# Moving the later gate columns behind the weight conversion in a fused mLSTM and bilinear kernel

## The chip, the cores and the metric

The kernel runs on one core of a Trainium2 chip. The number that counts is the device time of one execution in microseconds (us). The kernel before takes 566.85 us, the median of three runs (566.21 to 568.91).

The engines are named as in the profile: PE (matrix multiplications), DVE, ACT and POOL (elementwise work), and SP, whose queue issues the DMAs here. Each engine works through its own list of instructions in order; semaphores make one wait for another.

## The reference

Two steps are fused. The first is a recurrent attention with exponential gates over 4 batch rows, 8 heads, 768 time steps and a head size of 40. The second takes its output as 3072 tokens of 320 numbers through a bilinear layer with 1536 hidden columns.

```python
for t in range(S):
    m_new = np.maximum(f_gate[:, :, t] + m, i_gate[:, :, t])
    f_stab = np.exp(f_gate[:, :, t] + m - m_new)
    i_stab = np.exp(i_gate[:, :, t] - m_new)
    C = f_stab * C + i_stab * outer(v_t, k_t)
    n = f_stab * n + i_stab * k_t
    y_t = sigmoid(o_gate_t) * (C @ q_t) / max(|n . q_t|, 1)
x = y as (3072, 320)
out = (x @ w_a * (x @ w_b)) @ w_out
```

The three weight matrices arrive as 64-bit floats, everything else as 32-bit floats.

## The kernel before

**Chunks.** Time is cut into six pieces of 128 steps. A chunk is one piece of one batch row, so there are 24; chunk n is piece n // 4 of batch row n % 4. Within a chunk the recurrence is a masked matrix product: scores from q and k (`pS`), multiplied by a decay matrix E (tile `gbc`), times v (`pV`); from piece 1 on, the state that earlier pieces left (`cst`) is added (`pI`, `num`). The state is brought up to date by `weigh` (POOL: v times a column of weights w, tile `vw`) and `stage_u` (PE: `pU`). `stage_f` divides and applies the output gate (tile `osig`), and `stage_d` transposes the result (`pX`) into `xh` and `xl`, a high and a low part, which the bilinear layer reads.

**Gates.** `first_gates` works out the gate sums of the first 128 columns, at the kernel's start. `later_gates` does columns 128 to 767: a scan for the running maximum, three elementwise passes over 32 x 640 numbers, five scans for the running sums G, the tables beta and w, transposes on PE (`ptg`) into `gtab`, an Exp over part of it, and `dec`. G also goes to DRAM (`g_dram`), from which `load_g` spreads one chunk's rows over 128 partitions as the raw E of chunks 4 and later; POOL masks it (`affine_select`), and ACT takes eight Exps with a column of `gtab` as bias (`stage_e`). Chunks 0 to 3 build E on PE instead (`begin_e`, `pE`) and need no `gtab`, except for the column w in `weigh`.

**Weights.** The 64-bit weights come in 32 pieces ("stages" x = 0 to 31). For each one ACT makes a high part (`high`), DVE a low part (`low`) and their union (`join`), ACT rounds it (`lead_part`), and DVE subtracts (`low_part`): three DVE and two ACT instructions, or one more of each for the pieces 4, 12, 20 and 28. Hidden columns come in 12 groups ff; group ff needs eight stages for every three groups (`need`).

**Blocks.** The bilinear layer takes the chunks in nine blocks of two or three chunks. A block is twelve times `up(ff)` (16 matmuls into two `pu` accumulators) and `down(ff)` (three matmuls per chunk into `pd`), with g, gh and gl between them on DVE, ACT and POOL. `run_block(kb)` writes block kb's matmuls and in between, at a pace set by `units` over `total`, the attention of the chunks that block kb + 1 needs. During block 0 the conversion of the stages 5 to 31 is written too, one step for every four matmuls.

**What sets the order.** Chunks 0 and 1 and the stages 0 to 4 are written out by hand. Blocks 0 and 1 are ordered for all engines by the scheduler at build time; from block 2 on, PE and SP follow the written order. In `rest()` the written order is: two steps of `later_gates`, the transposes and E of chunk 2, the rest of `later_gates`, then `weigh` and `stage_u` of chunks 0 and 1, then the attention.

## Time and profile before

| | |
|---|---|
| runs | 568.91, 566.21, 566.85 us; median 566.85 |
| profiled execution | 564.22 us |
| its span, from the first to the last instruction | 562.4 us |
| mean granted PE clock | 0.969 of full speed |
| busy: PE, DVE, ACT, POOL | 534.6, 411.9, 221.3, 126.6 us |

The profile gives for each instruction its start, its length and, where the engine was idle before it, for how long and what released it. Matmul ends are modelled, so that a stretch can count as busy on PE though its clock was low; the granted clock stands beside it.

### The profile page before, as it was taken

The page shows a single profiled execution, that of the slowest core. Times are in us where ns is not written, and L with a number is a line of the kernel's source. Part 1 is how long each engine was busy: PE and PEld are TensorE (multiplying, and loading weights), DVE is VectorE, ACT ScalarE, POOL GpSimd, SP SyncE. Part 2 cuts the span into 40 slices and gives each one's busy share as a digit, 9 for nine tenths or more (in the row PEclk, how much of TensorE's full clock was granted, in tenths as well). Part 3 has the DMA queues.
Part 4 walks back from the last instruction along what each step waited for, and adds up shares of the span by engine and source line. Part 5 has one row for each costly group of instructions (what it writes and reads, how often), then busy time and mean ns, then how long its engine had stood idle before and what let it go on. Part 6 is the DMA issues. An engine that isn't in the chain of part 4 may idle for free.

```text
span 562.4 us, 12436 instructions
## 1 busy us (share of the span) xinstructions
PE 534.6 (95%) x4810; PEld 505.9 (90%) x4810; DVE 411.9 (73%) x967; ACT 221.3 (39%) x530; POOL 126.6 (23%) x185
## 2 busy tenths in 40 slices
PE   9678799997999999999999999999999999899997
PEld 6576699997999989999899999899999999799997
DVE  6899976468879965978859995978859577744342
ACT  5677854344422642332632441541432515111111
POOL 2012245253331230332132231233030202100000
PEclk9587789999999999999999999999999999999999
DMA  9999513567956955677855654967544834200001
GB/s 172 300 273 303 110 38 89 117 95 160 153 135 105 167 119 76 146 142 158 139 119 119 120 108 106 190 121 155 89 122 75 139 76 114 35 1 24 2 0 36
DMA packets 198679, 66.77 MB, mean 119 GB/s; under 512 B 184252, under 2 KB 191900, under 8 KB 198620
## 3 DMA queue, kind: packets, MB, share of 16 engines
q1 hardware_dynamic: 198620, 65.98, 57.8%
q8 instruction: 38, 0.62, 0.5%
q14 instruction: 21, 0.17, 0.1%
HBM read 41.11 MB, written 5.97 MB: 84 GB/s over the span
## 4 chain that ended last, share of the span: by engine, by line
PE 68%; DVE 5%; DMA 5%; issue 4%; ACT 3%; SPq 2%; POOL 1%; POOLq 0%; ACTq 0%; DVEq 0%
PE pu L744 39%; PE pd L716 18%; PE pV L520 3%; PE pS L468 2%; PE pU L544 2%; DMA osig<-in_o_gate_dram 1%; ACT gbc L413 1%; PE pX L630 1%; PE pS L818 1%; PE pI L494 1%; PE pV L870 1%; DMA T<-qks 1%; SPq L160 1%; DMA gbc<-g_dram 1%; DMA qk<-in_q_dram 1%
## 5 line engine op out<-in xcount | busy, mean ns | idle before, releaser
L744 PE MATMUL pu<-xh,w 128*128 128x384 f32 (+1 forms) x1080 | 282.5, 328 | 3.9 <-DVE w L373 2.2
L744 PE MATMUL pu<-xl,w 128*128 128x384 f32 (+1 forms) x648 | 210.7, 327 | 1.0 <-DVE xl L636 1.0
L744 PEld LDWEIGHTS pu<-xh,w 128*128 128x128 f32 x1080 | 194.1, 192 | 7.1 <-DVE w L373 3.4
L716 PE MATMUL pd<-w,gh 128*128 128x320 f32 x576 | 132.8, 315 | 1.0 <-ACT gh L754 1.0
L744 PEld LDWEIGHTS pu<-xl,w 128*128 128x128 f32 x648 | 124.7, 193 | 2.0 <-DVE xl L636 1.3
L716 PEld LDWEIGHTS pd<-w,gh 128*128 128x128 f32 x576 | 97.9, 190 | 1.6 <-ACT gh L754 1.2
L752 DVE TENSOR_TENSOR g<-pu,g 128x384 f32<-128x384 f32 (+1 forms) x108 | 54.6, 505 | 56.7 <-PE pu L744 53.7
L716 PE MATMUL pd<-w,gl 128*128 128x320 f32 x288 | 89.2, 315 | 0.0
L751 ACT COPY g<-pu 128x384 f32<-128x384 f32 (+1 forms) x92 | 40.5, 440 | 114.4 <-PE pu L744 114.1
L413 ACT ACTIVATE gbc<-gbc,gtab 128x128 f32<-128x128 f32 x160 | 49.4, 389 | 23.8 <-POOL gbc L406 23.8
L455 POOL TENSOR_TENSOR vr<-va 128x336 f32<-128x336 f32 x18 | 14.0, 775 | 187.1 <-PE pV L520 176.6
L716 PEld LDWEIGHTS pd<-w,gl 128*128 128x128 f32 x288 | 53.8, 189 | 0.0
L756 DVE TENSOR_TENSOR gl<-g,gh 128x384 fp32r<-128x384 f32 (+1 forms) x92 | 50.3, 546 | 1.6
L754 DVE CAST gh<-g 128x384 fp32r<-128x384 f32 (+1 forms) x96 | 32.7, 341 | 1.6
L475 ACT CAST pb<-gbc 128x512 bf16<-128x512 f32 x36 | 22.2, 616 | 26.7 <-DVE gbc L473 26.6
L527 DVE TENSOR_TENSOR num<-pV,num 128x336 f32<-128x336 f32 x18 | 9.1, 504 | 29.9 <-PE pV L520 29.9
L406 POOL TENSOR_SCALAR_AFFINE_SELECT gbc<-gbc 128x1024 f32<-128x1024 f32 x20 | 23.7, 1185 | 18.9 <-DMA gbc<-g_dram 17.1
L562 ACT CAST cb<-cst 128x168 bf16<-128x168 f32 x18 | 6.0, 331 | 54.6 <-DMA gbc<-g_dram 26.7
L473 DVE TENSOR_TENSOR gbc<-pS,gbc 128x512 f32<-128x512 f32 x36 | 24.5, 680 | 3.6 <-PE pS L468 3.6
L520 PEld LDWEIGHTS <-pb 128*128 128x128 bf16 x576 | 23.1, 96 | 4.2 <-DVE pb L479 1.8
L607 POOL TENSOR_TENSOR osig<-osig,den 128x320 f32<-128x320 f32 x22 | 17.0, 771 | 43.8 <-DVE den L602 25.4
L431 ACT CAST qks<-qk 128x320 bf16<-128x320 f32 x36 | 16.1, 452 | 27.3 <-DMA T<-qks 12.4
(130 smaller groups left out, 814.1 us busy)
## 6 DMA issues: line engine op xcount, KB each, us to landing
gbc<-g_dram SPq DMA_DIRECT2D x20, 512.0 KB
qk<-in_q_dram SPq DMA_DIRECT2D x24, 160.0 KB
qk<-in_k_dram SPq DMA_DIRECT2D x24, 160.0 KB
va<-in_v_dram SPq DMA_DIRECT2D x24, 160.0 KB
osig<-in_o_gate_dram SPq DMA_DIRECT2D x24, 160.0 KB
raw<-in_moe_w_out_dram SPq DMA_DIRECT2D x12, 320.0 KB
out_dram<-o SPq DMA_DIRECT2D x24, 160.0 KB
raw<-in_moe_w_a_dram SPq DMA_DIRECT2D x8, 384.0 KB
```

The costliest lines, as they stand in the source:

```text
L406: nc.gpsimd.affine_select(E, E, pattern=[[0, H], [1, P]], compare_op=ALU.is_ge, fill=-1e30, base=0, channel_multiplier=-1,)
L413: nc.scalar.activation(E[:, h], E[:, h], AF.Exp, bias=beta[:, h:h + 1])
L473: nc.vector.tensor_tensor(E, pS, E, op=ALU.mult)
L475: nc.scalar.copy(pb[:, 0], E)
L520: nc.tensor.matmul(pv[:, h], pb[i][:, h % HH, :], vb[j][:, h], start=(x == 0), stop=(x == len(terms) - 1),)
L607: (nc.vector if n < NS else nc.gpsimd).tensor_tensor(yv, yv, den.unsqueeze(2).broadcast_to([P, H, D]), op=ALU.mult)
L716: nc.tensor.matmul(pd[t][:, 0:DM], a[:, cols], w, start=(ff == 0 and first), stop=(ff == NF - 1 and last),)
L744: up_in = nc.tensor.matmul(acc[j], a, r, start=(x == 0), stop=(x == len(terms) - 1),).ins
L751: (nc.vector.tensor_copy if kb > 0 and ff in [1, 2] else nc.scalar.copy)(g, acc[0])
L752: nc.vector.tensor_tensor(g, acc[1], g, op=ALU.mult)
L754: (nc.vector.tensor_copy if kb > 0 else nc.scalar.copy)(gh, g)
L756: (nc.gpsimd if kb * 12 + ff < 16 else nc.vector).tensor_tensor(gl, g, gh.bitcast(F32), op=ALU.subtract)
```

## The change

The column w of chunks 0 to 3 gets a small table of its own, `w0tab` (128 x 32), worked out in the hand-written part by `first_weights`: one DVE add, one PE transpose, one Exp on ACT. With it `weigh` of chunks 0 and 1 is written before block 0, into two buffers of the tag `vr`, which is idle until chunk 6; `weigh` of the other early chunks uses the same two buffers instead of the single buffer `vw`. `later_gates` leaves `rest()` and is written at the head of chunk 3 in `early_chunk`, after stage 25 of the conversion (`need(26)`), with `load_g` of chunk 4 behind it. It no longer handles the first piece: no copies of its two rows on ACT, five pieces to DRAM instead of six, five transposes instead of six; the Exp over `gtab` is split in two, a small one for piece 1's decay column a and one for the rest. The Sigmoids of two output gates move into chunk 2. Block 0 writes a conversion step for every three matmuls, and starts its attention eight units later.

```diff
+    w0tab = wpool.tile([P, BH], F32, name="w0tab")
...
+    def first_weights():
+        w0 = gf[:, 0:P]
+        nc.vector.tensor_scalar(w0, gb3[0][:, 1], gb3[0][:, 0, P - 1:], None, op0=ALU.add)
+        pw = ps_dn.tile([P, 512], F32, tag="pd2", name="pw")[:, 0:BH]
+        nc.tensor.transpose(pw, w0, ident[0:BH, 0:BH])
+        nc.scalar.activation(w0tab, pw, AF.Exp)
...
-        with tc.issue_after(start["dve"]):
+        with tc.issue_after(after["dve"]):
             nc.vector.tensor_tensor_scan(m, f, i, gm[:, P - 1:P], op0=ALU.add, op1=ALU.max)
...
-        with tc.issue_after(start["act"]):
-            nc.scalar.copy(G[:, 0], gb3[0][:, 0])
-            nc.scalar.copy(tab[BH:2 * BH, 0], gb3[0][:, 1])
...
-            nc.sync.dma_start(g_dram.rearrange("c g t -> g c t"), G)
+            nc.sync.dma_start(g_dram[1:].rearrange("c g t -> g c t"), G[:, 1:])
...
-            for c in range(n3):
+            cs = range(max(half * n3, 1), (half + 1) * n3)
+            for x, c in enumerate(cs):
...
+        nc.scalar.activation(a_col(1, 0, B), a_col(1, 0, B), AF.Exp)
+        x = gtab[:, 4 * BH:].rearrange("p (c g) -> p c g", g=3 * BH)[:, :, 0:2 * BH]
         nc.scalar.activation(x, x, AF.Exp)
...
     def w_col(c, b):
-        return g_col(c, b, 1)
+        return g_col(c, b, 1) if c > 0 else w0tab[:, b * H:(b + 1) * H]
...
     def early_chunk(n):
+        if n == NS + 1:
+            need(26)
+            yield from later_gates()
+            load_g(NE)
         aside("L", n)
...
         yield from (begin_e if n + 1 < NE else stage_e)(n + 1)
+        if n == NS:
+            for b in range(NS, B):
+                squash(0, b, 1)
...
-        vw = apool.tile([P, H, DV], F32, tag="vw", name=f"vw{n}", bufs=1)
+        vw = apool.tile([P, H, DV], F32, tag="vr", name=f"vw{n}")
...
         run(E[1], 2)
+        first_weights()
...
+        for n in range(NS):
+            weigh(n)
...
     def rest():
-        gates = later_gates()
-        for _ in range(2):
-            next(gates)
-            yield
-        yield from begin_a(NS)
-        yield from begin_e(NS)
-        yield from gates
         for n in range(NS):
-            weigh(n)
             yield from stage_u(n)
             if n == 0:
                 with tc.issue_after(issued["w"]):
                     load(NS + 1)
-        for b in range(2, B):
-            squash(0, b, 1)
-        load_g(NE)
+        yield from begin_a(NS)
+        yield from begin_e(NS)
         yield from attention()
...
+        lead_in = 8 if kb == 0 else 0
+        acc = -lead_in
...
-            if x % (4 if kb == 0 else 6) == 0:
+            if x % (3 if kb == 0 else 6) == 0:
                 next(conv, None)
-            acc += units / (total * (0.93 if kb < 2 else 0.88))
+            acc += (units + lead_in) / (total * (0.93 if kb < 2 else 0.88))
```

Three places show what this does to the order on the engines. The line numbers of the changed kernel are higher by five to twelve; the operations are the same.

**DVE at the start of block 0**, while the stages 5 to 9 are converted (`cw` and `w`: conversion; `T_1`: the copy of chunk 2's transposed k; `qks_91`: the gate rows; `g_0`: block 0). Before:

```order
L220 TENSOR_TENSOR qks_91<-qks_91 32x640
L222 TENSOR_TENSOR qks_91<-qks_91 32x640
L354 SCALAR_TENSOR_TENSOR cw<-qks_89,cw 128x320
L354 SCALAR_TENSOR_TENSOR cw<-qks_90,cw 128x320
L354 SCALAR_TENSOR_TENSOR cw<-qks_89,cw 128x384
L373 TENSOR_TENSOR w_473<-cw,w_473 128x320
L808 COPY T_1_492<-pT_1_493 128x512
L221 TENSOR_TENSOR qks_91<-qks_91 32x640
L752 TENSOR_TENSOR g_0_470<-pu_0_1_449,g_0_470 128x256
```

Now:

```order
L359 SCALAR_TENSOR_TENSOR cw<-qks_90,cw 128x320
L359 SCALAR_TENSOR_TENSOR cw<-qks_89,cw 128x320
L359 SCALAR_TENSOR_TENSOR cw<-qks_90,cw 128x320
L359 SCALAR_TENSOR_TENSOR cw<-qks_89,cw 128x384
L378 TENSOR_TENSOR w_474<-cw,w_474 128x320
L820 COPY T_1_590<-pT_1_591 128x512
L764 TENSOR_TENSOR g_0_478<-pu_0_1_458,g_0_478 128x256
L378 TENSOR_TENSOR w_489<-cw,w_489 128x320
```

The elementwise passes over 32 x 640 gate numbers are gone from here. They now stand among the conversion of the last stages, and the five scans for G stand behind the subtraction of stage 29 (`w_983`), with two subtractions of the conversion still to come:

```order
L229 TENSOR_TENSOR qks_91<-qks_91 32x640
L359 SCALAR_TENSOR_TENSOR cw<-qks_89,cw 128x320
L378 TENSOR_TENSOR w_957<-cw,w_957 64x384 x2
L359 SCALAR_TENSOR_TENSOR cw<-qks_90,cw 128x320
L378 TENSOR_TENSOR w_983<-cw,w_983 128x320
L233 SCALAR_TENSOR_TENSOR qks_92<-one,qks_91 32x128 x5
L641 TENSOR_TENSOR xl_1041<-pX_1042,xh_1040 128x3x128
L820 COPY T_1_1117<-pT_1_1118 128x512
```

**POOL at the end of block 0** (`gl`: low part of g of one group; `osig`: output gate of chunk 2 or 3 times the reciprocal; `gbc`: the mask on a loaded E). Before, the mask there is that of chunk 5:

```order
L756 TENSOR_TENSOR gl_8_1194<-g_8_1159,gh_8_1192 128x256
L607 TENSOR_TENSOR osig_159<-osig_159,den_1122 128x320
L406 AFFINE_SELECT gbc_1022<-gbc_1022 128x1024
L756 TENSOR_TENSOR gl_9_1257<-g_9_1238,gh_9_1255 128x256
L455 TENSOR_TENSOR vr_1619<-va_86 128x336
```

Now it is that of chunk 4 (`gbc_1005`), and the output gate of chunk 3 and the last `gl` of block 0 stand behind it:

```order
L768 TENSOR_TENSOR gl_10_1299<-g_10_1286,gh_10_1297 128x256
L398 MEMSET qks_91 128x8x8 x2
L411 AFFINE_SELECT gbc_1005<-gbc_1005 128x1024
L612 TENSOR_TENSOR osig_160<-osig_160,den_1179 128x320
L768 TENSOR_TENSOR gl_11_1330<-g_11_1317,gh_11_1328 128x256
L411 AFFINE_SELECT gbc_1103<-gbc_1103 128x1024
```

The rows moved are the masks of chunks 4 and 5. In the kernel before, chunk 4's stands far earlier, between gl_3 and the weighted v of chunk 1.

**PE and ACT at the change from block 0 to block 1** (`pd`: block 0's `down`; `pu_0_0`: block 1's first accumulator; `pI`, `pX`, `pT`: attention). PE before:

```order
L716 MATMUL pd_0_446<-w_1243,gh_10_1294 128x320 x2
L716 MATMUL pd_0_446<-w_1243,gl_10_1296 128x320
L716 MATMUL pd_1_447<-w_1243,gh_10_1294 128x320 x2
L716 MATMUL pd_1_447<-w_1243,gl_10_1296 128x320
L805 MATMUL pT_0_1395<-ident,qk_82 128x128 x3
L744 MATMUL pu_0_0_1355<-xh_933,w_302 128x256
L805 MATMUL pT_0_1395<-ident,qk_82 128x128
L744 MATMUL pu_0_1_1356<-xh_933,w_435 128x256
```

PE now:

```order
L728 MATMUL pd_1_456<-w_1031,gh_11_1328 128x320 x2
L830 MATMUL pS_1_1199<-T_0_1105,T_1_1117 128x128 x4
L728 MATMUL pd_0_455<-w_1031,gl_11_1330 128x320
L728 MATMUL pd_1_456<-w_1031,gl_11_1330 128x320
L260 MATMUL ptg<-ident,qks_92 128x96 x3
L270 MATMUL pdec<-ends,sides 128x64
L851 MATMUL pI_0_1222<-cst_93,T_0_1105 128x42 x4
L851 MATMUL pI_1_1223<-cst_93,T_0_1105 128x42 x4
L635 MATMUL pX_1243<-ident,osig_160 128x128 x3
L549 MATMUL pU_1152<-vw_1127,qk_80 64x42 x8
L817 MATMUL pT_0_1398<-ident,qk_82 128x128 x4
L756 MATMUL pu_0_0_1358<-xh_1040,w_303 128x256
```

Before, block 1's first `up` matmuls stand ahead of the last `pd` rows, and `pI` of chunk 4 and `pX` of chunk 3 further ahead still. Now `pu_0_0` stands behind the whole of block 0, the transposes of the gate table, `pI` and `pX`. ACT before, around chunk 5's Exps (`gbc_1022`) and the cast of chunk 3's `xh`, which block 1 reads:

```order
L413 ACTIVATE gbc_1022<-gbc_1022,gtab 128x128 x8
L751 COPY g_10_1283<-pu_10_0_1273 128x256
L431 CAST qks_91<-qk_81 128x8x40
L754 CAST gh_10_1294<-g_10_1283 128x256
L634 CAST xh_933<-pX_1206 128x3x128
L751 COPY g_11_1314<-pu_11_0_1304 128x256
L754 CAST gh_11_1325<-g_11_1314 128x256
```

ACT now:

```order
L266 ACTIVATE gtab<-gtab 128x32
L418 ACTIVATE gbc_1005<-gbc_1005,gtab 128x128 x8
L436 CAST qks_91<-qk_81 128x8x40
L418 ACTIVATE gbc_1103<-gbc_1103,gtab 128x128 x2
L738 COPY o_0_1350<-pd_0_455 128x320
L418 ACTIVATE gbc_1103<-gbc_1103,gtab 128x128
L738 COPY o_1_1353<-pd_1_456 128x320
L418 ACTIVATE gbc_1103<-gbc_1103,gtab 128x128 x4
L268 ACTIVATE gtab<-gtab 128x4x64
L418 ACTIVATE gbc_1103<-gbc_1103,gtab 128x128
L274 ACTIVATE dec<-pdec 128x64
L639 CAST xh_1040<-pX_1243 128x3x128
```

The cast of chunk 3's `xh` now stands behind the eight Exps of chunk 4 (`gbc_1005`), the eight of chunk 5 (`gbc_1103`), block 0's output copies and the Exps of the gate tables.

More of the change, by code (lines that the diff above doesn't have):

```diff
@@ L245, in later_gates @@
         nc.vector.tensor_tensor(
-            tab[2 * BH:], tab[BH:2 * BH], G[:, :, P - 1:P].broadcast_to([BH, NC, P]), op=ALU.add
+            tab[2 * BH:, 1:], tab[BH:2 * BH, 1:], G[:, 1:, P - 1:P].broadcast_to([BH, NC - 1, P]),
+            op=ALU.add,
         )
@@ L251, in later_gates @@
             n3 = NC // 2
-            for c in range(n3):
+            cs = range(max(half * n3, 1), (half + 1) * n3)
+            for x, c in enumerate(cs):
                 nc.tensor.transpose(
-                    pt[:, c * 3 * BH:(c + 1) * 3 * BH], tab[:, half * n3 + c, :],
-                    ident[0:3 * BH, 0:3 * BH],
-                )
-            n0, n1 = (BH, n3 * 3 * BH) if half == 0 else (0, (n3 * 3 - 1) * BH)
-            nc.vector.tensor_copy(
-                gtab[:, half * (n3 * 3 - 1) * BH:][:, 0:n1 - n0], pt[:, n0:n1]
-            )
+                    pt[:, x * 3 * BH:(x + 1) * 3 * BH], tab[:, c, :], ident[0:3 * BH, 0:3 * BH]
+                )
+            n1 = (len(cs) * 3 - half) * BH
+            nc.vector.tensor_copy(gtab[:, (3 * cs[0] - 1) * BH:][:, 0:n1], pt[:, 0:n1])
             yield
-        x = gtab[:, BH:].rearrange("p (c g) -> p c g", g=3 * BH)[:, :, 0:2 * BH]
+        nc.scalar.activation(a_col(1, 0, B), a_col(1, 0, B), AF.Exp)
+        x = gtab[:, 4 * BH:].rearrange("p (c g) -> p c g", g=3 * BH)[:, :, 0:2 * BH]
         nc.scalar.activation(x, x, AF.Exp)
@@ L270, in later_gates, with g_col @@
         yield
-    def g_col(c, b, x):
-        return gtab[:, (3 * c + x) * BH + b * H:][:, 0:H]
+    def g_col(c, b, x, nb=1):
+        return gtab[:, (3 * c + x) * BH + b * H:][:, 0:nb * H]
     def beta_col(c, b):
@@ L278, in w_col, with a_col @@
     def w_col(c, b):
-        return g_col(c, b, 1)
-    def a_col(c, b):
-        return g_col(c - 1, b, 2)
+        return g_col(c, b, 1) if c > 0 else w0tab[:, b * H:(b + 1) * H]
+    def a_col(c, b, nb=1):
+        return g_col(c - 1, b, 2, nb)
     def weight_stages():
@@ L1015, in run_block @@
         done = False
-        acc = 0.0
+        lead_in = 8 if kb == 0 else 0
+        acc = -lead_in
         total = NF * (16 + 3 * sizes[kb])
```

## The prediction

> **What bounds the kernel now.** I read the page, then a table of busy time by stretch, then the timeline of each engine where PE loses time.
>
> The page's line of 40 slices (14 us each, busy tenths of PE) and the table of stretches (columns: length; busy PE, weight loads, DVE, ACT, POOL; granted clock, DMA share, GB/s):
>
> ```profile
> PE   9678799997999999999999999999999999899997
> ...
> 20.00:30.00 10.00, 5.67 (x23) 4.74 (x23) 8.95 (x18) 6.07 (x16) 0.00 (x0) 0.50 1.15 273
> 30.00:40.00 10.00, 9.03 (x78) 8.30 (x79) 9.03 (x22) 8.37 (x17) 0.22 (x1) 0.86 1.04 305
> 40.00:50.00 10.00, 7.55 (x50) 5.70 (x49) 9.75 (x20) 6.13 (x15) 2.64 (x6) 0.99 1.04 325
> 50.00:60.00 10.00, 8.78 (x58) 7.55 (x58) 10.00 (x25) 8.15 (x20) 2.30 (x5) 0.66 0.94 226
> 60.00:70.00 10.00, 8.01 (x54) 7.51 (x56) 8.64 (x20) 8.77 (x24) 3.50 (x4) 0.68 0.50 84
> ...
> 90.00:100.00 10.00, 10.00 (x76) 9.26 (x75) 4.04 (x11) 4.88 (x15) 4.70 (x6) 1.00 0.29 60
> ...
> 120.00:130.00 10.00, 8.07 (x80) 7.56 (x79) 3.81 (x14) 1.45 (x4) 2.63 (x5) 1.00 0.94 170
> 130.00:140.00 10.00, 8.96 (x106) 8.37 (x106) 9.97 (x23) 5.79 (x18) 4.25 (x6) 1.00 0.66 130
> ```
>
> From the twelfth slice on, 154 us, PE is busy nearly throughout: it is the bound there, and the change leaves that part alone. What can move is the time at which block 1 begins, and the little that PE waits in block 1. Between 20 and 70 us PE is idle for about 11 of 50 us, and its clock is 0.50 to 0.86 in most of it, while DVE is busy for 46 of the 50: it converts weights for which block 0 waits. From 90 to 100 us DVE has 6 us to spare and PE has none. So gate work on DVE costs time before 60 us and is cheap after 90.
>
> These are the gate's DVE instructions between 26 and 60 us (groups by line; busy us, mean ns):
>
> ```profile
> L228 DVE TENSOR_TENSOR_SCAN qks<-one,qks 32x128 f32<-32x128 f32 x5 | 1.7, 389 | 0.0
> L218 DVE TENSOR_TENSOR_SCAN qks<-qks 32x640 f32<-32x640 f32 x1 | 1.5, 1542 | 0.0
> L245 DVE TENSOR_TENSOR qks<-qks 32x768 f32<-32x768 f32 x1 | 1.0, 951 | 0.0
> L258 DVE COPY gtab<-ptg 128x256 f32<-128x256 f32 x2 | 0.8, 415 | 0.0
> L220 DVE TENSOR_TENSOR qks<-qks 32x640 f32<-32x640 f32 x1 | 0.8, 817 | 0.0
> L222 DVE TENSOR_TENSOR qks<-qks 32x640 f32<-32x640 f32 x1 | 0.8, 815 | 0.0
> L243 DVE TENSOR_TENSOR qks<-qks,qks 32x640 f32<-32x640 f32 x1 | 0.8, 815 | 0.0
> L221 DVE TENSOR_TENSOR qks<-qks 32x640 f32<-32x640 f32 x1 | 0.8, 814 | 0.0
> ```
>
> Together 8.2 us.
>
> **The change part by part.** First term: how much earlier is stage 12 converted, which block 0's group 3 waits for?
>
> ```profile
> 30.00 1.09 PE L805 MATMUL pT<-ident,qk 128*128 128x128 f32 x4 [2.24 <-DMA qk<-in_q_dram]
> ...
> 32.79 0.68 DVE L808 COPY T<-pT 128x512 f32<-128x512 f32 x1
> ...
> 38.63 0.56 DVE L373 TENSOR_TENSOR w<-cw,w 128x384 fp32r<-128x384 f32 x1 [0.72 <-ACT w L367]
> ...
> 39.84 1.28 DVE L824 TENSOR_TENSOR gbc<-pS,gbc 128x512 f32<-128x512 f32 x2
> ...
> 49.41 0.55 DVE L373 TENSOR_TENSOR w<-cw,w 64x384 fp32r<-64x384 f32 x1
> ```
>
> Not all 8.2. The scan L218 and two passes stand ahead of the copy of chunk 2's transposed k. That copy waits for two sets of four transposes whose data lands at 30.00; the first takes 1.1 us, so both end near 32.4, and the copy can start 0.4 us earlier and no more. Behind it, up to stage 12's last subtraction (end 49.96), stand one pass (0.8), the five scans (1.7), two table passes (0.8 + 1.0) and one copy (0.4): 4.7 us. The decay product of chunk 2 (1.28) now stands behind stage 12, and the wait of 0.72, in which ACT was late behind a table load, goes. 49.96 - 0.4 - 4.7 - 1.3 - 0.7 gives **stage 12 at about 42.9 us, 7 earlier**.
>
> Second term: when do the gates come instead? The scans for G stand behind the subtraction of stage 29, two from the last.
>
> ```profile
> 62.31 0.55 DVE L373 TENSOR_TENSOR w<-cw,w 64x384 fp32r<-64x384 f32 x1 [0.98 <-ACT w L367]
> ...
> 72.60 0.49 DVE L610 TENSOR_TENSOR osig<-pV,osig 128x320 f32<-128x320 f32 x1 [2.18 <-POOL osig L607]
> ...
> 88.44 0.47 DVE L373 TENSOR_TENSOR w<-cw,w 128x320 fp32r<-128x320 f32 x1
> ```
>
> From 49.96 to the end of the last subtraction, 88.91, DVE needs 39.0 us. To the end of the scans it now has the two last subtractions less (0.8), one gate copy (0.4), one k copy (0.7) and small state work less that now stands behind them (I take 1.1, the rest of what the rows list there), the product of chunk 2 more (1.3), and the gate scan, three passes and five scans more (5.6). Two waits should go: 0.98 (ACT was in chunk 4's Exps, now later) and 2.18 (POOL's product with osig stood behind a weighted v that waited for the one buffer vw; there are two now). 39.0 - 0.8 - 2.2 + 1.3 + 5.6 - 3.2 = 39.7, so **the scans end at S = 82.6 us**. Most of the 7 us is handed back here.
>
> Third term: what hangs on the scans. Before, E of chunk 4 is ready long before its use, and nothing waits for it. Now the chain behind S decides when block 1 starts, since its first accumulator stands in PE's row behind pI of chunk 4 and pX of chunk 3, and its xh behind both chunks' Exps on ACT. Rows for the links:
>
> ```profile
> 81.02 0.69 SPq L581 DMA_DIRECT2D c_dram<-cb  x2
> 83.01 0.79 SPq L587 DMA_DIRECT2D cx<-c_dram  x2
> ...
> 87.25 0.35 SPq L180 DMA_DIRECT2D gbc<-g_dram  x1
> ...
> 90.21 0.72 POOL L607 TENSOR_TENSOR osig<-osig,den 128x320 f32<-128x320 f32 x1 [0.69 <-DVE den L602]
> 91.52 1.09 POOL L406 TENSOR_SCALAR_AFFINE_SELECT gbc<-gbc 128x1024 f32<-128x1024 f32 x1 [0.58 <-DMA gbc<-g_dram]
> ...
> 92.64 2.45 ACT L413 ACTIVATE gbc<-gbc,gtab 128x128 f32<-128x128 f32 x8 [0.41 <-POOL gbc L406]
> ...
> 99.16 0.48 ACT L634 CAST xh<-pX 128x384 fp32r<-128x384 f32 x1 [2.21 <-PE pX L630]
> ...
> 107.28 0.73 ACT L726 COPY o<-pd 128x320 f32<-128x320 f32 x2
> ```
>
> The write of G to DRAM: 2.4 us from S to the next issue on SP (c_dram to cx: 2.0, and the issue). The load of E: 87.25 to 91.5, 4.3. The mask 1.1. Then POOL multiplies chunk 3's osig (0.7), and DVE its last product (0.49) and the gate copy (0.41), behind which ACT's Exps wait: 1.6. The small Exp (0.3, near the 0.31 of one of the eight), eight Exps (2.45), the cast for chunk 7 (0.4, a little under that of xh), eight Exps of chunk 5 (2.45), two output copies (0.7), two more Exps (0.7), the cast of xh (0.5), and 0.7 to the first matmul: 8.2. Sum 2.4 + 4.3 + 1.1 + 1.6 + 8.2 = 17.6, so **block 1 starts at about 100.2**. Before:
>
> ```profile
> 102.16 0.37 PE L744 MATMUL pu<-xh,w 128*128 128x256 f32 x1
> ...
> 104.56 0.46 PE L716 MATMUL pd<-w,gl 128*128 128x320 f32 x2
> ```
>
> At 102.16, but six matmuls of block 0 (the last pd, about 0.9 us) came after it: as if at 103.1. **The start of block 1 moves by -2.9 us.**
>
> Fourth term, the clock. By its order PE has 48 matmuls of block 0 and some 20 others left at S, about 7 us at the 19 in 2 us of the last row here, and then waits until S + 17, with little in between.
>
> ```profile
> 64.00:66.00 2.00, 2.00 (x11) 2.00 (x11) 1.84 (x4) 2.00 (x7) 0.00 (x0) 0.50 0.97 158
> ...
> 72.00:74.00 2.00, 2.00 (x11) 2.00 (x10) 1.40 (x3) 1.42 (x5) 0.89 (x2) 0.55 0.48 82
> 74.00:76.00 2.00, 2.00 (x19) 1.99 (x17) 2.00 (x5) 0.72 (x3) 0.52 (x1) 1.00 0.08 18
> ```
>
> After an idle time that ended at 62 (its row stands below) the clock was 0.50 from 64 to about 73.8 (0.55 in the slice before 74): nearly 10 us at half, 4.8 lost. That is the upper end; the lower is 0, if the gap is broken up enough. But PE waits 1.9 us from 120 to 130 and 1.0 from 130 to 140 for work that does not depend on its clock, so a late PE finds part of its waits gone. That leaves 0 to 1.9; I take 1.1. The Trainium skill (TensorE: Matmul & The Clock Gate, "What's actually happening") says that an idle window of about 3.4 us halves the clock and a busy one restores it: a rule against this change. By it the loss would be 1.7 us, an estimate, and the sum -1.2; by the row's full 4.8 the sum would be +1.9. The trace agrees on the half, not on the return, which took three times as long.
>
> Small parts. The early table w costs one DVE add (nearest row the 0.49 of a 128 x 320 product), one transpose and one Exp, ahead of a stretch in which PE is idle for 4.3 of 10 us (20 to 30) and waits for a load at its end: bounds 0 and 0.5, and I take 0, for the load hides it. Chunks 0 and 1 weighted early: before, the second stood behind chunk 4's mask on POOL and held PE up:
>
> ```profile
> 61.99 0.67 PE L544 MATMUL pU<-vw,qk 128*64 128x42 f32 x16 [3.19 <-POOL vw L854]
> ```
>
> That wait goes. But PE reaches the chain behind S early anyway, so it is worth 0 to 3.2, and I take 0; it would count only if the chain were not last. Two ACT copies and one piece of DRAM write less: nothing, ACT is idle for 4 of 10 us there.
>
> Sum: -2.9 + 1.1 = **-1.8 us**. Against the profiled execution's own 564.22 that is 562.4; against the median of the runs, which lies 2.6 higher, **565.0 us**.
>
> **The rivals.** *The lead survives (A).* If the conversion, no longer squeezed, runs with fewer of the stretched DVE instructions that the stretch from 50 to 90 us shows, S comes sooner:
>
> ```profile
> L373 DVE TENSOR_TENSOR w<-cw,w 128x384 fp32r<-128x384 f32 x8 | 5.1, 653 | 0.0
> ```
>
> The same subtraction took 0.56 at 38.63, without POOL beside it. The stages 13 to 31 have 57 such instructions; at 0.1 us each some 5 us are stretch. Against it: POOL has the same work in the new order. S = 77.6 gives -6.8: 560.0 us.
>
> *The boundary costs more than it gives (B, slower).* Place: PE between the last pd of block 0 and pu_0_0 of block 1. If the waits of 0.98 and 2.18 on DVE stay, under other names, S is 85.8 and block 1 starts at 103.4; with the full 4.8 of clock the change is +5.1: 572.0 us. It decides from S + 17.6 plus the clock loss above 103.1. For it: every link of the chain is in the trace, and none is covered. Against it: PE idles less before S.
>
> *The change does not do what it says (C).* If the arrival of weights set the pace, taking gates from DVE would leave it waiting, and the time would be that of before, 566.9. For it: DMA shares of 0.94 and more until 60. Against it: DVE is busy for 10.00 of 10 us from 50 on, and hardly waits for a raw tile.
>
> **How the numbers follow.** Forecast 0.45, with its own range 561.5 to 568.5; A 0.25; B 0.20; C 0.10. 0.5% is 2.8 us, about what a measurement of this kernel can tell from no change. Faster by more: 0.16 of the forecast's 0.45, and nearly all of A, 0.24: 0.40. Slower by more: 0.19 of B and 0.04 of the rest: 0.23. Within: 0.37. The range goes from 558.0 (A, less its far end) to 572.0 (half of B); some 0.14 is left out.
>
> **What would show it.** Stage 12's last subtraction near 43 us; the scans (L233) ending near 83; POOL's mask of chunk 4 waiting for its DMA until about 89; PE idle some 8 us before pI of chunk 4 (L851), a clock of 0.50 behind it, and the first pu of block 1 near 100. I am wrong if that first pu comes before 96 or after 104, or if PE's waits in block 1 change by more than 2 us.

## The result and the profile after

The changed kernel takes **561.19 us** (median of four runs, 559.67 to 562.85), the kernel before 566.87 in the same session (566.21 to 568.91). The ratio is 0.9897, with a 95% interval of 0.9866 to 0.9927: faster by 5.7 us, between 4.1 and 7.6. The forecast was 565.0, 1.8 us faster. The ratios leave out runs more than 1.5% above the fastest run of the same kernel (three of twelve in run 9 below, one of six in run 10), and the medians hold all runs, so that the two can differ by some tenths of a per cent.

| | before | after |
|---|---|---|
| profiled execution, us | 564.22 | 559.67 |
| its span, us | 562.4 | 557.9 |
| mean granted PE clock | 0.969 | 0.974 |

First, where in the program the gain lies. Block n of the bilinear layer ends with its output copies, and SP issues the output's DMAs right behind them. The timeline of SP before, blocks 0 and 1:

```profile
107.71 0.84 SPq L727 DMA_DIRECT2D out_dram<-o  x2
...
160.80 0.84 SPq L727 DMA_DIRECT2D out_dram<-o  x2
```

and after:

```profile
93.93 0.97 SPq L739 DMA_DIRECT2D out_dram<-o  x2
...
156.67 0.85 SPq L739 DMA_DIRECT2D out_dram<-o  x2
```

At the end of block 1 the changed kernel is 4.1 us ahead, of 4.55 between the two profiled executions, and it is the same 4.1 at the end of block 2 (221.93 after, 226.07 before). So the first 157 us hold the difference. Block 0's outputs moved by 13.8 us, which measures nothing: before, the start of block 1 stands ahead of block 0's last `pd` on PE; now it stands behind it.

The row of 70 to 80 us of before, and then the table of stretches of after (columns as in the prediction: length; busy PE, weight loads, DVE, ACT, POOL; granted clock, DMA share, GB/s):

```profile
70.00:80.00 10.00, 10.00 (x85) 9.40 (x86) 6.97 (x16) 5.24 (x16) 3.66 (x5) 0.81 0.15 27
```

```profile
20.00:30.00 10.00, 6.37 (x39) 5.46 (x40) 8.94 (x21) 6.72 (x19) 0.00 (x0) 0.63 1.10 274
30.00:40.00 10.00, 9.82 (x81) 8.39 (x81) 6.95 (x15) 7.40 (x17) 2.24 (x3) 0.83 1.05 315
40.00:50.00 10.00, 9.84 (x104) 9.12 (x104) 9.91 (x23) 9.34 (x25) 2.25 (x3) 1.00 1.03 328
50.00:60.00 10.00, 8.86 (x65) 8.28 (x66) 9.87 (x20) 8.06 (x20) 3.33 (x4) 1.00 1.07 190
60.00:70.00 10.00, 10.00 (x68) 9.52 (x68) 9.94 (x23) 5.53 (x14) 2.49 (x2) 0.83 0.65 86
70.00:80.00 10.00, 6.63 (x44) 5.79 (x43) 9.76 (x20) 4.00 (x10) 1.79 (x5) 0.93 0.00 1
80.00:90.00 10.00, 9.70 (x70) 9.29 (x68) 8.31 (x21) 2.60 (x8) 5.15 (x10) 0.90 0.50 136
90.00:100.00 10.00, 7.94 (x62) 7.12 (x63) 4.96 (x11) 8.19 (x28) 5.26 (x9) 0.78 0.56 112
100.00:110.00 10.00, 10.00 (x92) 9.56 (x92) 5.79 (x18) 4.91 (x8) 3.53 (x6) 0.87 0.61 129
...
120.00:130.00 10.00, 7.20 (x75) 6.67 (x74) 6.56 (x15) 2.26 (x7) 5.70 (x7) 1.00 0.89 154
130.00:140.00 10.00, 8.64 (x115) 7.90 (x115) 9.97 (x25) 4.68 (x14) 3.22 (x4) 1.00 0.84 139
```

Read the PE column first. From 20 to 50 us PE is idle for 4.0 us, where it was 7.75 before: the earlier conversion gives 3.8 us. From 50 to 100 it is idle for 6.9, where it was 3.2: 3.7 go back, most of it from 70 to 80, where DVE does the moved gate work: there PE waits for a product with `osig` that stands on DVE behind two of the gate passes.

```profile
76.35 0.41 PE L635 MATMUL pX<-ident,osig 128*128 128x128 f32 x2 [2.54 <-DVE osig L615]
```

Then the clock: from 50 to 80 the busy time times what is missing to full clock is 2.2 us here; before, by the prediction's rows and the one above, it was 7.4. From 80 to 110 it is 4.0 here and nothing before. So PE's idle time did not change, and its half-clock time moved from ahead of the chain to beside and behind it. It also became less: in slices of 2 us, from the start to the end of block 1, the clock costs 11.6 us, and 13.9 before. That is 2.3 of the 4.1 us; the idle time gives 0.1 (18.6 and 18.7), and the other 1.7 are busy time at full clock, of which these rows say no more.

Now the chain that the prediction made the bound, link by link, in the timelines of after (start, length, engine and line, operation, and in brackets the idle time ahead of it with its releaser):

```profile
42.48 1.14 DVE L378 TENSOR_TENSOR w<-cw,w 64x384 fp32r<-64x384 f32 x2
...
80.21 1.67 DVE L233 TENSOR_TENSOR_SCAN qks<-one,qks 32x128 f32<-32x128 f32 x5
...
83.64 1.59 SPq L181 DMA_DIRECT2D gbc<-g_dram  x2
...
87.47 1.09 POOL L411 TENSOR_SCALAR_AFFINE_SELECT gbc<-gbc 128x1024 f32<-128x1024 f32 x1 [0.92 <-DMA gbc<-g_dram]
88.53 0.73 POOL L612 TENSOR_TENSOR osig<-osig,den 128x320 f32<-128x320 f32 x1
...
89.30 0.49 DVE L615 TENSOR_TENSOR osig<-pV,osig 128x320 f32<-128x320 f32 x1 [1.57 <-POOL osig L612]
89.70 0.35 DVE L264 COPY gtab<-ptg 128x192 f32<-128x192 f32 x1
...
90.08 0.23 ACT L266 ACTIVATE gtab<-gtab 128x32 f32<-128x32 f32 x1
90.22 2.43 ACT L418 ACTIVATE gbc<-gbc,gtab 128x128 f32<-128x128 f32 x8
...
96.30 0.47 ACT L639 CAST xh<-pX 128x384 fp32r<-128x384 f32 x1
...
96.45 1.09 PE L549 MATMUL pU<-vw,qk 128*64 128x42 f32 x16 [1.16 <-ACT dec L274]
...
98.24 0.99 PE L756 MATMUL pu<-xh,w 128*128 128x256 f32 x3
```

Stage 12 is converted at 43.62, the scans for G end at 81.88, and the first matmul of block 1 comes at 98.24, 16.4 us behind them. POOL and DVE wait at each hand-over in between, and ACT runs without a gap from 90.08 on.

In block 1 the waits stayed, and the longest is for the DMA transposes of chunk 6. PE's waits from 98 to 156 us of after (who waits for what: total us, times, longest):

```profile
PE pS L473 <- DMA T<-qks: 1.6, 1, 1.6
PE pI L499 <- DVE gbc L478: 1.0, 1, 1.0
```

Before, from 102 to 160:

```profile
PE pS L468 <- DMA T<-qks: 1.9, 2, 1.5
PE pI L494 <- DVE gbc L473: 1.0, 1, 1.0
```

### The profile page after: what moved, and what is told of

Its sections match the earlier page's. It is cut to its first block, busy times and chain, and to the rows that moved or that the text cites. A ratio compares the mean times of both kernels' runs of the same rounds, so it can differ in the third digit from the quotient of the medians.

```text
span 557.9 us, 12440 instructions
## 1 busy us (share of the span) xinstructions
PE 530.3 (95%) x4810; PEld 503.1 (90%) x4810; DVE 413.7 (74%) x968; ACT 218.6 (39%) x528; POOL 126.5 (23%) x185
## 4 chain that ended last, share of the span: by engine, by line
PE 61%; DVE 11%; SPq 7%; ACT 6%; DMA 6%; issue 6%; POOL 2%; POOLq 0%; ACTq 0%; DVEq 0%
PE pu L756 35%; PE pd L728 17%; PE pV L525 3%; SPq L336 3%; ACT gbc L418 2%; PE pS L473 2%; DMA gbc<-g_dram 1%; PE pU L549 1%; DMA raw<-in_moe_w_a_dram 1%; SPq L149 1%; DMA raw<-in_moe_w_out_dram 1%; DVE g L764 1%; DVE w L378 1%; PE pX L635 1%; DVE gbc L482 1%
## 5 line engine op out<-in xcount | busy, mean ns | idle before, releaser
L728 PE MATMUL pd<-w,gh 128*128 128x320 f32 x576 | 131.1, 312 | 0.0
L763 ACT COPY g<-pu 128x384 f32<-128x384 f32 (+1 forms) x92 | 40.3, 440 | 116.5 <-PE pu L756 116.1
L411 POOL TENSOR_SCALAR_AFFINE_SELECT gbc<-gbc 128x1024 f32<-128x1024 f32 x20 | 23.3, 1164 | 16.6 <-DMA gbc<-g_dram 13.2
L482 DVE TENSOR_TENSOR gbc<-gbc,pb 128x512 f32<-128x512 f32 x36 | 25.1, 698 | 2.0 <-ACT pb L480 2.0
```

The source lines that it names most:

```text
L411: nc.gpsimd.affine_select(E, E, pattern=[[0, H], [1, P]], compare_op=ALU.is_ge, fill=-1e30, base=0, channel_multiplier=-1,)
L482: nc.vector.tensor_tensor(E, E, pb[:, 0], op=ALU.subtract)
L728: nc.tensor.matmul(pd[t][:, 0:DM], a[:, cols], w, start=(ff == 0 and first), stop=(ff == NF - 1 and last),)
L763: (nc.vector.tensor_copy if kb > 0 and ff in [1, 2] else nc.scalar.copy)(g, acc[0])
```

## The experiments

Two readings were open. By the first, the time lies where the gates went: conversion first, scans at the end, chain behind them. By the second, the moved gates bring nothing, and what the prediction priced at zero brings the gain: the early weighted values, and block 0's pace (a conversion step for every three matmuls, and a lead-in: the attention starts eight units later). The first four runs take these apart. The runs of the kernel before differ from session to session, so each ratio is against those beside it.

**1. Only the small table and the early weighted values** (the kernel before, with `first_weights`, `w0tab`, the tag `vr`, and `weigh` ahead of block 0):

```diff
+        first_weights()
...
+        for n in range(NS):
+            weigh(n)
...
         for n in range(NS):
-            weigh(n)
             yield from stage_u(n)
```

> The kernel before with only the small table of w and the early weighted values of chunks 0 and 1; the gate work for later columns stays ahead of the conversion. Theory 1 (the gain is DVE's lead in the conversion, as far as the chain behind the scans lets it through): stage 12's last subtraction stays near 50 us and the first pu of block 1 near 101 to 102; 565.5 to 567, so 0 to -1.4 us. Rival 1 (the gain is the wait of pU for vw, 3.19 us, that goes): the first pu of block 1 near 98 to 99 and 561 to 563.5.

Measured 562.54 us, ratio 0.992 (0.9894 to 0.9947): 4.5 us from a part that the prediction priced at nothing, within the range of rival 1. The early start of block 1 that rival 1 expects does not show: the profiled execution is the slowest of the six (564.17), its block 1 starts at 104.19 and ends at 160.41, where before it ended at 160.80. Where the other runs gain their time is not shown.

**2. The change without its pace:**

```diff
-        lead_in = 8 if kb == 0 else 0
+        lead_in = 0
...
-            if x % (3 if kb == 0 else 6) == 0:
+            if x % (4 if kb == 0 else 6) == 0:
```

> The changed kernel with the old pacing (every fourth matmul, no steps held back). The gates still stand behind stage 26. Theory 1: stage 12 near 43 to 44 us, scans near 82, block 1 near 98; 560 to 562.5, within 1.5 us of the changed kernel. Rival 2: 565 to 567.

Measured 562.27, ratio 0.9916 (0.9891 to 0.9941), against 0.9897 for the whole change: the intervals overlap. In its profile the scans end 1.9 us later and block 1 starts 1.7 us later than in the changed kernel:

```profile
82.11 1.67 DVE L233 TENSOR_TENSOR_SCAN qks<-one,qks 32x128 f32<-32x128 f32 x5
...
99.94 0.99 PE L756 MATMUL pu<-xh,w 128*128 128x256 f32 x3
```

The chain is 16.2 us here and 16.4 there, so block 1 follows the scans in both. The pair does not prove it, for here the whole conversion is later: stage 12 is converted at 46.43, against 43.62.

**3. Only the pace, on the kernel before:**

```diff
-        acc = 0.0
+        lead_in = 8 if kb == 0 else 0
+        acc = -lead_in
...
-            if x % (4 if kb == 0 else 6) == 0:
+            if x % (3 if kb == 0 else 6) == 0:
...
-            acc += units / (total * (0.93 if kb < 2 else 0.88))
+            acc += (units + lead_in) / (total * (0.93 if kb < 2 else 0.88))
```

> The kernel before with only the pacing of the change: a conversion step after every third matmul of block 0 in place of every fourth, and the attention's first eight steps held back. Theory 1: the gates' DVE work stands where it stood, stage 12's last subtraction moves by under 1 us, block 1 starts within 1.5 us of 102; 565.5 to 568. Rival 2 (the gain is the faster pacing of the conversion, and the gates' place does nothing): block 1 near 98, 561 to 563.

Measured **556.12**, ratio 0.9805 (0.9775 to 0.9836): this part alone gives more than the whole change, and more than either reading expected.

**4. The change with the gates put back** at the head of `rest()`:

```diff
-        with tc.issue_after(after["dve"]):
+        with tc.issue_after(start["dve"]):
...
-        if n == NS + 1:
-            need(26)
-            yield from later_gates()
-            load_g(NE)
...
+        gates = later_gates()
+        for _ in range(2):
+            next(gates)
+            yield
+        yield from begin_a(NS)
+        yield from begin_e(NS)
+        yield from gates
...
-        yield from begin_a(NS)
-        yield from begin_e(NS)
+        load_g(NE)
```

> The changed kernel with the later gates back ahead of chunk 2's begin, and all else as changed (table of w, early weighted values, pacing). Theory 1: stage 12 near 49 to 50 us, the load of E long before its use, no PE idle time ahead of pI of chunk 4, block 1 near 101 to 103; 564.5 to 567.5. Rivals 1 and 2 (the early values or the pacing carry the gain): 560 to 562.

Measured **555.04** (553.96 to 555.71), ratio 0.9785 (0.9756 to 0.9815): faster than both kernels, and than any expectation. The move that gives the change its name costs about 6 us (0.9897 against 0.9785), and the first reading falls. Where does it cost? Block 1 starts at 96.99 here, 1.3 us before the changed kernel's, and its outputs leave at 151.53, 5.1 us before. So nearly 4 us are lost inside block 1. Its table of stretches:

```profile
120.00:130.00 10.00, 10.00 (x102) 9.71 (x101) 8.60 (x21) 5.22 (x15) 1.94 (x2) 1.00 0.84 189
130.00:140.00 10.00, 10.00 (x148) 9.61 (x147) 8.40 (x21) 4.06 (x13) 5.65 (x7) 1.00 0.67 132
```

PE does not wait at all where the changed kernel waits for 4.2 us. The order of DVE shows why. `r_0` is what is left of chunk 6's q after rounding to bf16, the first step toward its transposes; `g_0` and `g_1` are block 1's first two groups. In the changed kernel it reads (rows between are left out):

```
L764 TENSOR_TENSOR g_0_1381<-pu_0_1_1359,g_0_1381 128x256
...
L820 COPY T_1_1406<-pT_1_1407 128x512
...
L764 TENSOR_TENSOR g_1_1440<-pu_1_1_1419,g_1_1440 128x256
L440 TENSOR_TENSOR r_0_1580<-qk_80,qks_89 128x320
```

With the gates back:

```
L440 TENSOR_TENSOR r_0_1580<-qk_80,qks_89 128x320
...
L760 TENSOR_TENSOR g_0_1381<-pu_0_1_1359,g_0_1381 128x256
L820 COPY T_1_1406<-pT_1_1407 128x512
...
L760 TENSOR_TENSOR g_1_1440<-pu_1_1_1419,g_1_1440 128x256
```

`r` and `cr`, what is left of the state after rounding, share one tag with two buffers. In the written order chunk 6's `r` takes its buffers behind `cr` of chunk 4, which needs chunk 4's state matmuls `pU`, which need `vw` of chunk 4, which needs the gate table. With late gates these matmuls fall into block 1, and DVE waits ahead of the second `r` (that of k) for POOL's last reading of `cr` (`cb`). The rows of the changed kernel:

```profile
105.63 0.67 PE L549 MATMUL pU<-vw,qk 128*64 128x42 f32 x16
...
107.59 0.59 DVE L440 TENSOR_TENSOR r<-qk,qks 128x320 f32<-128x320 f32 x1
...
111.96 1.07 DVE L440 TENSOR_TENSOR r<-qk,qks 128x320 f32<-128x320 f32 x1 [0.63 <-POOL cb L574]
...
114.72 1.36 SPq L450 DMA_TRANSPOSE T<-qks  x1
...
117.24 4.59 SPq L450 DMA_TRANSPOSE T<-qks  x3
```

and with the gates back, where chunk 4's `pU` comes in pieces until 80.47:

```profile
80.16 0.31 PE L549 MATMUL pU<-vw,qk 128*64 128x42 f32 x2
...
97.10 0.48 DVE L440 TENSOR_TENSOR r<-qk,qks 128x320 f32<-128x320 f32 x1
...
107.40 7.22 SPq L450 DMA_TRANSPOSE T<-qks  x4
```

The transposes start 7.3 us earlier, and the wait of `pS` for them is gone. Runs 5 and 6 test from both sides whether the late state is the cause. That it acts through the shared buffer is read from the code and from that wait of 0.63 us; no run gives `r` and `cr` buffers of their own.

**5. Run 4 with chunk 4's state forced late**, behind the third matmul of block 1's second group:

```diff
+                    if (kb, ff, j) == (1, 1, 0) and x == 2:
+                        after["g1"] = up_in
...
-            nc.tensor.matmul(
-                pu[r:r + 64, x], nat(n)[0][:, 1, h, :], s["vw"][:, h], start=True, stop=True
-            )
+            with tc.issue_after(after["g1"]) if n == NF32 - 2 else nullcontext():
+                nc.tensor.matmul(
+                    pu[r:r + 64, x], nat(n)[0][:, 1, h, :], s["vw"][:, h], start=True, stop=True
+                )
```

> The kernel e4_gates_back with one order changed: the eight state matmuls of chunk 4 (L549 there, pU) stand on PE behind the third matmul of block 1's second accumulator, near where the changed kernel has them. Theory 2 (the four us in block 1 come from chunk 4's state update: its rest cr and chunk 6's first residual r share a buffer, so r, its transposes by DMA and the scores of chunk 6 follow late): block 1's start stays near 97, its end goes from 151.5 to about 155.5; 558.5 to 560. Rival 3 (moving the gates costs through DVE's work and the clock before block 1): nothing of that is changed here, so 554.5 to 556.

Measured 560.42 (556.89 to 563.14), ratio 0.989 (0.985 to 0.993): 5.4 us slower than run 4, and as slow as the change. The rows and then PE's waits from 100 to 155:

```profile
107.38 0.67 PE L551 MATMUL pU<-vw,qk 128*64 128x42 f32 x16
...
109.33 0.58 DVE L441 TENSOR_TENSOR r<-qk,qks 128x320 f32<-128x320 f32 x1
...
116.94 1.35 SPq L451 DMA_TRANSPOSE T<-qks  x1
...
PE pS L474 <- DMA T<-qks: 2.0, 2, 1.7
```

One edit of eight matmuls brings back the late `r`, the late transposes and the waits. It is not all clean: in this profile block 1 also starts later (first output of block 0 at 103.21, against 98.31 in run 4), after a wait of 3.2 us for a load of q that comes ahead of anything the edit moves. Of the 7.2 us between the two profiles 4.9 lie ahead of block 1 (it starts at 101.87, against 96.99) and 2.4 in it; there PE idles 4.1 us more, while run 4 loses 1.7 to its clock. So the size of 5.4 is for the medians, the mechanism is for the rows, and what the late state costs by itself is settled no closer than that.

**6. The kernel before with chunk 4's state early:** the same eight matmuls under `high_priority`, so that all stand in block 0 (before, five of the eight are in block 1):

```diff
+            with tc.high_priority() if n == NF32 - 2 else nullcontext():
```

> The kernel before with one order changed: the eight state matmuls of chunk 4 (pU), of which the last stands behind block 1's second group in the kernel before, all stand in block 0. Theory 2: chunk 6's transposes by DMA near 110 to 112 us in place of 119.5, PE's waits from 120 to 150 gone, block 1's start unchanged near 102; 562 to 564. Rival 3 (the gain of the early values and of the pacing is the conversion's): 566 to 568.

Measured 565.97 (12 runs), ratio 1.0005 (0.998 to 1.0029): no gain, and near rival 3's 566 to 568. PE's idle time from 100 to 155 us fell from 4.3 to 2.2, but in this profile the clock took it back: the loss from 20 to 100 rose from 12.8 to 15.4 us. It rose ahead of 76 us, and the moved matmuls stand at 83, so that it is not shown to come from the edit. The transposes of chunk 6 came only at 115.16: on SP the outputs of block 0 (108.98) and three loads stood ahead of them, and from 112.1 SP waited again, by the profile for a matmul of PE. So late state is enough to cause the waits; early state alone is not enough to gain.

**7 and 8. The pace in two halves**, on the kernel before. Only every third matmul:

```diff
-            if x % (4 if kb == 0 else 6) == 0:
+            if x % (3 if kb == 0 else 6) == 0:
```

> The kernel before with a conversion step after every third matmul of block 0, and nothing else. Theory 2: chunk 6's residual stands ahead of block 1's groups in DVE's order, as in e3_pace, so block 1 loses its waits; with the start of e3_pace 556, with the start of the kernel before 563. If the faster conversion is worth nothing by itself, 561 to 564; if it brings block 1 forward as in e3_pace, 555 to 558.

Measured 562.06, ratio 0.9924 (0.9895 to 0.9953). Only the lead-in of eight units:

```diff
-        acc = 0.0
+        lead_in = 8 if kb == 0 else 0
+        acc = -lead_in
...
-            acc += units / (total * (0.93 if kb < 2 else 0.88))
+            acc += (units + lead_in) / (total * (0.93 if kb < 2 else 0.88))
```

> The kernel before with the attention's first eight steps held back in block 0 and the conversion step after every fourth matmul, as before. Theory 2: chunk 6's residual stands ahead of block 1's groups in DVE's order too, so 561 to 564 if the held steps do nothing else; 555 to 558 if they, and not the faster conversion, bring block 1's start forward. Rival 3: 566 to 568.

Measured 557.73, ratio 0.9835 (0.9804 to 0.9866). The lead-in is the largest single piece, 8 to 9 us. In its profile all of chunk 4's state stands ahead of block 1 (its last `pU` at 82.39), chunk 6's transposes start at 111.84, and PE idles for 0.4 us in block 1. PE waits more from 50 to 60 than before, and yet its clock is better in the stretch behind:

```profile
50.00:60.00 10.00, 6.76 (x56) 6.17 (x55) 8.68 (x21) 5.40 (x14) 3.11 (x5) 0.86 0.76 192
60.00:70.00 10.00, 9.05 (x101) 8.04 (x100) 8.60 (x15) 9.03 (x26) 4.51 (x5) 0.97 0.70 122
```

**9. One word on the kernel before:** the weighted values in two buffers instead of one, with no early `weigh`:

```diff
-        vw = apool.tile([P, H, DV], F32, tag="vw", name=f"vw{n}", bufs=1)
+        vw = apool.tile([P, H, DV], F32, tag="vr", name=f"vw{n}")
```

> The kernel before with one line changed: the early weighted values of chunks 0 to 5 take two buffers in place of one; the table of w stays in the gates, nothing is issued earlier by hand. Theory 5 (the single buffer of weighted values is what held PE up at 62 us, with a stretch at half clock behind it, and what put chunk 4's last state matmul behind block 1's second group): pU's wait of 3.19 us goes, seven of chunk 4's eight state matmuls stand ahead of block 1 and the last at its start, PE's waits in block 1 fall from 4.4 to under 2 us; 559 to 563. Rival (the table of w and the early issue carry the gain of e1_early_w): 565.5 to 567.5.

Measured 564.28 (557.89 to 569.44, 12 runs), ratio 0.9925 (0.9895 to 0.9954): 2.5 us by the medians, 4.3 by the ratio; the median lies between the two expectations. By either count more than half of what run 1 gains comes with the second buffer. The wait of 3.19 us for `vw` is gone, but the clock is not better for it (13.5 us lost from 20 to 100, 12.8 before); the idle time in block 1 fell from 4.3 to 2.5.

**10. Run 4 with every fourth matmul again:**

```diff
-            if x % (3 if kb == 0 else 6) == 0:
+            if x % (4 if kb == 0 else 6) == 0:
```

> The kernel e4_gates_back with the conversion step after every fourth matmul again; the eight held steps, the table of w and the early weighted values stay. If the held steps are what the pacing brings, as e9_lead_in against e3_pace suggests: 554 to 557. If the faster conversion carries it once the values are early: 560 to 563.

Measured 555.35 (551.70 to 560.33), ratio 0.9784 (0.9747 to 0.9821): the same as run 4. Beside the lead-in the faster conversion adds nothing that the intervals show.

**11. The gates in the middle**, after stage 12 instead of 25:

```diff
-            need(26)
+            need(13)
```

> The changed kernel with the gates asked for behind stage 13 in place of 26; by its order the scans for G then stand eight conversion stages earlier on DVE. Five of chunk 4's eight state matmuls still stand behind block 1's first accumulators. Theory 6 (late gates cost twice: by the chain from the scans to block 1's first matmul, 16 to 17 us, and by chunk 4's late state update in block 1): scans end near 73, the chain is no longer last, block 1 starts near 95 to 97, but PE still waits some 4 us in block 1; 557.5 to 560.5. Rival (the chain is all that late gates cost): 554 to 556.5. Rival (the place of the gates doesn't matter): 561 to 562.

Measured 565.60 (560.52 to 568.19, 12 runs that fall into two groups, four at 560.5 to 561.9 and the others above 565.4), ratio 0.9956 (0.9926 to 0.9986). No expectation held. The scans end at 68.5, so the chain is no longer last; and PE's waits in block 1 are 1.9 us, not 4. PE's waits for the conversion are 2.1 us in all, as before (2.2). But from 88 to 105 PE runs at half clock, with no idle time on record from 88 on:

```profile
90.00:100.00 10.00, 10.00 (x42) 9.11 (x42) 4.95 (x12) 4.54 (x16) 5.42 (x8) 0.50 0.14 31
100.00:110.00 10.00, 10.00 (x65) 9.36 (x64) 2.90 (x8) 4.68 (x8) 1.03 (x2) 0.75 0.51 99
```

Block 0's outputs leave at 106.50. Why the half clock lasts, and what the two groups are, stays open.

**12. The change with chunk 3's `stage_d` ahead of chunk 4's attention**, which then goes behind block 1's second matmul on PE: this takes chunk 4's product with the state out of the chain. ACT still has the Exps ahead of `xh`.

```diff
+        if n == NS + 2:
+            yield from stage_d(n - 1)
...
-        if n > NS:
+        if n > NS and n != NS + 2:
...
+            with tc.issue_after(after["up"]) if n == NS + 2 else nullcontext():
```

> The changed kernel with chunk 4's scores and its product with the state (begin_b, begin_i) moved behind chunk 3's output in PE's order, and behind block 1's second matmul. Chunk 4's state matmuls then come with block 1's first accumulators, ahead of its first group, and chunk 6's transposes by DMA all ahead of the next load of k. ACT still has the Exps of chunks 4 and 5 ahead of xh of chunk 3. Theory 6 (late gates cost by the chain up to block 1 and by chunk 4's late state update): the product of chunk 4 leaves the chain, so block 1 starts 0 to 3 us earlier than 98.2, and PE's waits in block 1 fall from 4.7 to under 2 us; 555 to 559. Rival (in the changed kernel block 1's waits have another cause than the late state): 560 to 562.

Measured 562.94 (561.74 to 569.49, 12 runs), ratio 0.996 (0.993 to 0.999), and 555 to 559 was expected. Block 1 starts at 96.63, only 1.6 us earlier, since PE now waits for other work of ACT (`osig`, `dec`) instead:

```profile
93.15 0.33 PE L636 MATMUL pX<-ident,osig 128*128 128x128 f32 x1 [1.62 <-ACT osig L618]
...
95.39 1.08 PE L550 MATMUL pU<-vw,qk 128*64 128x42 f32 x16 [1.92 <-ACT dec L275]
96.63 1.01 PE L759 MATMUL pu<-xh,w 128*128 128x256 f32 x3 [0.15 <-ACT xh L640]
```

What chunk 4 needs of PE then lies in block 1, at half clock until 104. PE's idle time in block 1 did fall, from 4.7 to 2.0 us, as expected, though chunk 6's transposes start only at 119.13; by the profile they wait there for `pI` on PE, which reads an earlier chunk's `T` in the same buffer. But block 1 ends at 159.01, 2.3 us later than in the changed kernel: up to there PE idles 1.0 us less and loses 2.6 more to its clock, 1.0 of that ahead of 20 us. So a shorter chain with less waiting did not help, and why the clock is worse is not shown.

Side by side, with PE's idle time and its clock loss (busy time times what is missing to full clock), summed from stretches of 2 us of each profile:

| kernel | median us | ratio | idle 20 to 100 | clock loss 20 to 100 | idle 100 to 155 |
|---|---|---|---|---|---|
| before | 566.87 | 1 | 11.0 | 12.8 | 4.3 |
| after | 561.19 | 0.9897 | 10.8 | 9.7 | 4.7 |
| 1 early values | 562.54 | 0.992 | 11.4 | 12.6 | 1.5 |
| 2 no pace | 562.27 | 0.9916 | 10.9 | 12.0 | 4.8 |
| 3 pace | 556.12 | 0.9805 | 13.2 | 5.4 | 0.3 |
| 4 gates back | 555.04 | 0.9785 | 10.0 | 7.3 | 0.5 |
| 5 state late | 560.42 | 0.989 | 13.3 | 10.1 | 4.6 |
| 6 state early | 565.97 | 1.0005 | 10.2 | 15.4 | 2.2 |
| 7 every third | 562.06 | 0.9924 | 9.7 | 15.8 | 1.8 |
| 8 lead-in | 557.73 | 0.9835 | 13.4 | 6.8 | 0.4 |
| 9 two buffers | 564.28 | 0.9925 | 10.8 | 13.5 | 2.5 |
| 10 gates back, every fourth | 555.35 | 0.9784 | 10.2 | 10.9 | 0.5 |
| 11 gates in the middle | 565.60 | 0.9956 | 10.2 | 12.9 | 1.9 |
| 12 `stage_d` first | 562.94 | 0.996 | 12.9 | 10.3 | 2.0 |

Every kernel at 558 or below idles for half a microsecond or less in block 1, and no other does. The idle time before block 1 does not tell the fast kernels from the slow ones. The waits in block 1 are not all of it, though. Summed from the start to the end of block 1, in one profile each, the clock costs 13.9 us before, 7.6 in run 3 and 7.4 in run 8, and the idle time is 18.7, 17.2 and 17.6. So what the pace brings there is clock, far more than waiting. Between the changed kernel and run 4 it is the other way round: idle time 18.6 and 14.9, clock 11.6 and 9.3.

## Why the prediction was right, and where it was off

**Stage 12**: 42.9 forecast, 43.6 measured. **The scans**: 82.6 forecast, 81.9 measured, and "Most of the 7 us is handed back here" held: 3.8 us of PE's idle time gained before 50 us, 3.7 back before 100.

**The chain** is the term that was mis-sized: "Sum 2.4 + 4.3 + 1.1 + 1.6 + 8.2 = 17.6" against 16.4. Three of its five links fit within 0.1 us: the mask 1.1, the step to ACT 1.5 for 1.6, the rest 8.2. The two that are DMAs were shorter: G to DRAM 1.8 (81.88 to 83.64) for 2.4, and the load of E 3.8 (to 87.47) for 4.3. With the scans 0.7 earlier, "The start of block 1 moves by -2.9 us" became -4.9 (103.1 to 98.24). Run 2 agrees that this start follows the scans (they are 1.9 us later there, and it is 1.7 later). But runs 11 and 12, which take the scans or chunk 4's product out of it with the gates still late, were not faster; in their profiles the clock costs more. So the chain rests on the rows of the traces, and what it costs is not shown by itself.

**The clock** term, +1.1 net behind the start: -4.9 at the start became -4.1 at the end of block 1, so +0.8. The half clock itself came in two pieces and was 4.0 us over 80 to 110, near the forecast's upper 4.8; but the statement "PE idle some 8 us before pI of chunk 4" was wrong. PE's rows of block 0 lasted to 91, its waits were spread over 70 to 100 (3.4, 0.3 and 2.1 us in the three stretches), and only some 2.1 of the 4.0 us fell behind the start (half clock from 98.24 to 102.5).

The sum of -1.8 us for the profiled execution thus became -4.55: 2.0 from the start, 0.3 from the clock, 0.4 behind block 1. The last 1.1 us of the miss in the median are the execution profiled before, 2.6 us below its median, where that of after is 1.5 below.

**PE's waits in block 1** stayed, as said (4.3 to 4.7 us). That was luck: in part at least they hang on chunk 4's state, of which the prediction says nothing. It is late in both kernels, before because of the order of chunk 4's `pU`, after because of the gate table. With the state early about half of the waits went before (2.2 us left in run 6).

**The zeros.** The early values ("I take 0; it would count only if the chain were not last") are worth 4.5 us in the kernel before, and the condition may be the reason that this did no harm: the chain is last in the changed kernel. No run takes the early values out of that kernel, so this is argued and not shown. The pace was never priced as a term; alone it is worth 10.9 us, and with the late gates about 1, which the intervals don't tell from nothing. What failed is the sentence that gate work on DVE "is cheap after 90". The work came to lie from 68 to 87, among the last of the conversion, where PE idled for 2.54 us behind it; and the gates' results come late for two others, the chain to block 1 and chunk 4's state. Together that cost more than the 3.8 us of idle time before 50. So the working holds for where block 1 starts, and not for where the gain comes from: the move, to which it credits the gain, costs some 6 us (run 4), and the parts that it put at nothing bring the gain.

**The rivals.** A (the lead survives) was right in the size, 560.0, and wrong in the cause: the scans did not come at 77.6. B did not happen: the scans ended well before its 85.8, and about half of the clock loss fell ahead of the start. C is excluded by stage 12, which did come 6.3 us earlier.

**Not settled.** Why the lead-in makes the clock return sooner; where the half clock of runs 11 and 12 comes from; whether `r` with a buffer of its own would end the waits in block 1; and why PE's waits for loads of q before 60 us add up to anything from 1.5 to 5.8 us in these profiles, which moves block 1's start.

## What to carry to other kernels

Moving work off a busy engine moves its results too: list who reads them, and price the chain behind the new place before the time that becomes free at the old one. If an edit bundles an order, a buffer and a pace, run each alone on the old kernel; here the part that gave the change its name was the one that cost time. A wait for a transfer in a later block can come from two tiles that share a tag: look in the order of instructions for the first step toward that transfer, and for whose buffer it takes.

## What the runs showed of the hardware that was not expected

The half clock came in stretches of very different length behind gaps of similar length. In run 8 PE idles for 3.2 us in all between 52 and 58; the clock is 0.50 from 57.3 to 60.7, so it is back after 3.4 us. Before, a gap of 3.19 us to 61.99 was followed by 0.89 from 62 to 64, where the clock fell at 63.5, and then by half clock to 73.8, for 10.2 us. The Trainium skill (TensorE: Matmul & The Clock Gate, "What's actually happening") gives an idle window and a busy window of about 3.4 us; the short case agrees, and the long one took three times that. In these traces the stretches are near whole multiples of the short one: 3.4 us also in run 4 (113.1 to 116.5) and in the changed kernel (61.5 to 64.9), 6.8 there from 95.7 to 102.5, and 17.0 in run 11 (88.0 to 105.0). In run 4 the clock also fell with PE recorded as busy throughout, and in run 11 with 0.35 us of idle time in the 2 us ahead. A slice of run 4:

```profile
114.00:116.00 2.00, 2.00 (x10) 1.98 (x10) 1.74 (x5) 0.71 (x2) 1.32 (x3) 0.50 0.97 186
```

Matmul ends are modelled in the profile, so that short idle times there may be hidden; no run here tells.
